# q of the first two units fetched two positions to a packet, with its decay factors in that order and ten more fillers on TensorE

## The chip, the core and the metric

The kernel runs on one core of a Trainium2 chip. A core has a matrix engine, TensorE (PE in the profile, its weight loads PEld), three engines for elementwise work, VectorE (DVE), ScalarE (ACT) and GpSimd (POOL), and SyncE (SP), which here only issues DMAs. Sixteen DMA engines move data between the chip's memory (HBM) and the core's on-chip memory of 128 rows (SBUF). TensorE writes its products to a second on-chip memory (PSUM), from where DVE or ACT take them. The engines run side by side and wait for one another on semaphores.

The metric is the device time in microseconds (us): the median of several runs. The profile is of one execution, and has times of its own.

## The reference

Two blocks follow one another. The first is a retention layer: for each of 8 batches and 8 heads, with 576 positions and 64 values to a head, scores are taken between q and k, multiplied by a decay and applied to v. The second is a gated feed-forward network without nonlinearity. All is float32.

```python
scores = scale * np.matmul(q, k.transpose(0, 1, 3, 2))        # scale = 1/sqrt(64)
gamma = 1.0 - 2.0 ** (-5.0 - np.arange(H))
Dmat = np.where(rel >= 0, gamma[:, None, None] ** rel, 0.0)   # rel = pos_i - pos_j
x = np.matmul(scores * Dmat, v)          # (8, 8, 576, 64), then laid out as (4608, 512)

a = x @ w1                               # 512 -> 1024
b = x @ w2
h = a * b @ w3                           # 1024 -> 1024
out = h @ w_out                          # 1024 -> 512
```

The weights come as float64 values. The kernel takes them as pairs of 32-bit integers and converts them itself.

## The kernel before, in words

**Units.** The retention is worked in units. A unit is a pair of batches and one piece of the positions; a pair has five pieces, the first of 64 positions and four of 128, so there are 4 x 5 = 20 units, numbered g. The decay gamma^(i-j) is split into a factor for q (`decay_q`, which has the scale in it) and one for k, which is applied to v (`decay_k`). Within a unit the full scores are computed and masked to j <= i; from earlier pieces comes a running state, k times v, kept in PSUM.

**The steps of a unit.** `load` (L87, its DMA at L93) fetches k, q or v of a unit into a tile with one position to each row of SBUF: a row holds, for 2 batches and 8 heads, 64 values, so every packet of the transfer is 64 values, 256 bytes. `scale` (L195, L204) multiplies q or v by its factor, on DVE, POOL or ACT. `front` (L207) turns k and q with PE transposes (L218), two heads at a time, into PSUM tiles `tp`, from which ACT copies (L221) them to `kT` and `qT`. `score` (L224) has PE compute the scores (L233), and DVE multiplies them by the mask (L236) into `pm`. `state` (L240) adds k times v on PE (L255), and ACT copies the state (L259). `pv_state` and `pv` (L264, L278) multiply q by the state (L274) and `pm` by v (L299); ACT copies the result (L306) into `xT`, the input of the network.

**The network.** `up` (L511) does the products with w1 and w2 by a scheme of seven products in place of eight (products at L528, sums on DVE at L533, the gate at L566). Its operands are sums of weights (`strassen_weights`, L149) and of tokens (`strassen_tokens`, L496). The weights are loaded in blocks (`load_block`, L342 and L345) and converted on ACT (L395 to L397) and DVE (L399, L402, L413, L426). w3 and w_out are multiplied together first (L477), and `down` (L632, L645) applies them. From about 200 us on the weights' sums are kept in HBM and fetched again for each group of tokens (`up2`, L1029, L1052).

**The order.** Each engine works its instructions off in the order in which the program writes them; nothing is rearranged. The tile framework adds the semaphore waits. Tiles come from pools with a fixed number of buffers, and a new tile waits until the buffer's last user is done. [...]The start of the program, which the change touches, is written out by hand: the loads of unit 0 (L97 to L100), the constants, the decay of q transposed to one position to each row (L117 to L125, tiles `dq`, `gps` and `gq`), then L726 to L770 with units 0 and 1, between them conversions of weights.

**Fillers.** `keep_busy(n)` (L127) issues n products of the identity with itself into a tile that nobody reads. A float32 product is two passes on PE, which the profile counts singly: 10 products at L119 are its x20.

Of the kernel before, what the change touches and what calls it, by code (L numbers as in the profile page):

```python
# [8 lines left out]
F32 = mybir.dt.float32  # L9
# [4 lines left out]
ALU = mybir.AluOpType  # L14
# [5 lines left out]
def kernel(  # L20
# [13 lines left out]
    nc = tc.nc  # L34
    moe_w1, moe_w2, moe_w3, moe_w_out = (
        w.bitcast(I32).rearrange("r (c t) -> r c t", t=2) for w in (moe_w1, moe_w2, moe_w3, moe_w_out))
    B, H, S, D = q.shape
# [3 lines left out]
    P = 128  # L41
# [6 lines left out]
    NC = (S + P - 1) // P  # L48
    short = S - (NC - 1) * P
    sizes = [short] + [P] * (NC - 1)  # L50
    starts = [0] + [short + c * P for c in range(NC - 1)]
    G = NB2 * NC
    NB = 3
    TB = S // NB
    NT = 2 * TB // P
    KD = DM // P
    KF = DF // P
# [4 lines left out]
    const = ctx.enter_context(tc.tile_pool(name="const", bufs=1))  # L62
    wp = ctx.enter_context(tc.tile_pool(name="wp", bufs=1))
    ffn = ctx.enter_context(tc.tile_pool(name="ffn", bufs=2))
# [6 lines left out]
    pools = {}  # L71
# [9 lines left out]
    acc = acc_part.enter_context(tc.tile_pool(name="acc", bufs=7, space=PSUM))  # L81
# [3 lines left out]
    live = {}  # L85

    def load(g, names, engine=nc.sync):  # L87
        i, c = divmod(g, NC)
        sz = sizes[c]
        src = {"k": k, "q": q, "v": v}  # L90
        for nm in names:
            t = pools["ld"].tile([P, 2 * H, D], F32, tag="ld_" + nm, name="ld_" + nm)
            engine.dma_start(  # L93
                t[:sz], src[nm][2 * i:2 * i + 2, :, starts[c]:starts[c] + sz, :].rearrange("b h p d -> p (b h) d"))
            live[nm, g] = t

    dq = ffn.tile([P, 4, 2, TB], F32, tag="c", name="dq", bufs=1).rearrange("p a b s -> p (a b s)")[:H, :S]  # L97
    nc.scalar.dma_start(dq, decay_q)
    load(0, "k")
    load(0, "q")  # L100

    ident = const.tile([P, P], F32, tag="ident", name="ident")
    make_identity(nc, ident)
# [19 lines left out]
    for c in (0, slice(1, NC)):  # L123
        n = short if c == 0 else P
        nc.vector.tensor_copy(gq[:n, c, :], gps[:n, c, :])  # L125

    def keep_busy(n):  # L127

        t = acc.tile([P, P], F32, tag="acc", name="idle")
        for _ in range(n):  # L130
            nc.tensor.matmul(t, ident, ident, start=True, stop=True)
# [63 lines left out]
    def scale(g, nm, scalar=False, engine=nc.gpsimd):  # L195
        c = g % NC
        sz = sizes[c]
        t, gam = live[nm, g], {"q": gq, "v": gk}[nm]
        t = t[:sz].rearrange("p (b h) d -> p b h d", b=2)
        if scalar:  # L200
            for h in range(H) if scalar is True else scalar:
                nc.scalar.mul(t[:, :, h, :], t[:, :, h, :], gam[:sz, c, h:h + 1])
            return
        engine.tensor_tensor(  # L204
            out=t, in0=t, in1=gam[:sz, c].unsqueeze(1).unsqueeze(3).to_broadcast([sz, 2, H, D]), op=ALU.mult)

    def front(g, names="kq"):  # L207
        c = g % NC
        sz = sizes[c]
        for nm in names:  # L210
            src = live[nm, g]
            dst = pools["fr"].tile([P, 2, NP, P], F32, tag=nm + "T", name=nm + "T",
                                   bufs=1 if nm == "k" and g >= NC else 2)
            for b in range(2):
                tp = acc.tile([P, NP, P], F32, tag="acc", name="tp")
                for p in range(NP):
                    h = b * H + 2 * p
                    nc.tensor.transpose(tp[:, p, :sz],  # L218
                                        src[:sz, h:h + 2, :].rearrange("p a d -> p (a d)"),
                                        ident[:sz, :sz])  # L220
                nc.scalar.copy(dst[:, b, :, :sz], tp[:, :, :sz])  # L221
            live[nm + "T", g] = dst

    def score(g):  # L224
        c = g % NC
        sz = sizes[c]
        kT, qT = live["kT", g], live["qT", g]
        pm = pools["fr"].tile([P, 2, 2, NP, P], F32, tag="pm", name="pm", bufs=1)
        for b in range(2):
            sc = [acc.tile([P, NP, P], F32, tag="acc", name="sc") for j in range(2)]  # L230
            for p in range(NP):
                for j, hs in enumerate(heads):
                    nc.tensor.matmul(sc[j][:sz, p, :sz], kT[hs, b, p, :sz], qT[hs, b, p, :sz],  # L233
                                     start=True, stop=True)
            for j in range(2):
                nc.vector.tensor_mul(pm[:sz, b, j, :, :sz], sc[j][:sz, :, :sz],  # L236
                                     mask[:sz, :sz].unsqueeze(1).to_broadcast([sz, NP, sz]))
        live["pm", g] = pm

    def state(g):  # L240
        c = g % NC
        sz = sizes[c]
        if c == NC - 1:
            return
        vs = live["v", g]
        kn = live["k", g]
        if c == 0:
            live["st"] = st_ps.tile([P, 2, NP, D], F32, tag="st", name="st")
        st = live["st"]

        for b in range(2):
            for p in range(NP):
                for j, hs in enumerate(heads):
                    h = b * H + 2 * p + j
                    nc.tensor.matmul(st[hs, b, p, :], kn[:sz, h, :], vs[:sz, h, :],  # L255
                                     start=(c == 0 and b == 0 and p == 0), stop=(c == NC - 2),
                                     skip_group_check=True)
        sb = pools["fr"].tile([P, 2, NP, D], F32, tag="sb", name="sb")
        nc.scalar.copy(sb, st)  # L259
        live["sb", g + 1] = sb  # L260
# [64 lines left out]
    def load_block():  # L325
        n = loaded[0]
        if n == len(blocks):
            return
        key, w = blocks[n]
        t = raw.tile([P, CV, 2], I32, tag="raw", name="raw", bufs=5)  # L330
        if key[0] in ("A", "w12"):
            if key[0] == "A":
                _, r, f = key
                t4 = t.rearrange("p (j c n) t -> p j c n t", j=2, c=2)
                parts = [(t4[:, j], w[:, f * P:(f + 1) * P]) for j, w in enumerate((moe_w1, moe_w2))]
            else:
                _, fp, _, r = key
                parts = [(t.rearrange("p (c n) t -> p c n t", c=2), w[:, fp * QC:(fp + 1) * QC])]
            for t2, src in parts:
                src = src[2 * r * P:2 * (r + 1) * P]  # L340
                if r == 0:
                    nc.sync.dma_start(t2, src.rearrange("(c p) n t -> p c n t", p=P))  # L342
                else:
                    for half in range(2):
                        nc.sync.dma_start(t2[heads[half]],  # L345
                                          src.rearrange("(c a d) n t -> a d c n t", a=2, d=D)[1 - half])
        elif key[0] == "wo":
            src = w.rearrange("(a i x) n t -> i a x n t", i=KF, x=BL)[key[1]]
            for a in range(QP):
                nc.sync.dma_start(t[a * BL:(a + 1) * BL], src[a])  # L350
        else:
            _, ft, h = key
            src = w[ft * P:(ft + 1) * P].rearrange("(j r) (a h f) t -> h a r j f t", r=BL, a=QP, h=DF // CV)
            for a in range(QP):
                nc.sync.dma_start(t[a * BL:(a + 1) * BL].rearrange("p (j f) t -> p j f t", j=P // BL), src[h, a])
        live["raw", n] = t
        loaded[0] += 1
# [105 lines left out]
    def convert(n):  # L463

        for _ in range(n):
            if go_on() is not None:
                return
# [105 lines left out]
    g = 0  # L573
# [152 lines left out]
    load_block()  # L726
    load(0, "v")
    load_block()
    load(1, "kq")
    load_block()  # L730
    load(1, "v")
    load_block()
    scale(0, "q", engine=nc.vector)
    front(0, "k")
    keep_busy(4)
    front(0, "q")
    convert(2)
    score(0)
    scale(0, "v")
    state(0)  # L740
    convert_up_to(1)
# [4 lines left out]
    convert_up_to(2)  # L746
    load_block()
    front(1, "k")
    keep_busy(4)
    scale(1, "q", engine=nc.vector)  # L750
    front(1, "q")
    convert(2)
# [392 lines left out]
    g = NC  # L1145
# [9 lines left out]
    for g in first_pair:  # L1155
        n = (1, 1, 2, 2)[g - NC]
# [38 lines left out]
    g = 2 * NC - 1  # L1195
# [10 lines left out]
    g = 2 * NC  # L1206
# [14 lines left out]
    for g in range(2 * NC, G):  # L1221
        n = dealt[g - 2 * NC]
# [42 lines left out]
    g = G  # L1265
# [44 lines left out]
```

## Time and profile before

Three runs took 835.63, 835.77 and 836.71 us; the median is 835.77. The profiled execution took 836.28 us by the same measure, of which 834.6 are the span of the profile.

| | busy us | share of the span | instructions |
|---|---|---|---|
| PE | 816.1 | 98% | 6095 |
| PEld | 735.5 | 88% | 6095 |
| DVE | 545.4 | 65% | 962 |
| ACT | 291.7 | 35% | 609 |
| POOL | 216.2 | 26% | 247 |

The core read 103.62 MB from HBM and wrote 22.28 MB. By stretches PE was busy for 25.38 us of the first 30, 27.25 of the next 30, 39.51 of the 40 after these, and 99.97 of the 100 from there. PE's mean clock was 0.994 of full over the span, and 0.83 in the first 30 us.

In the profile a line such as L233 is a line of the kernel before. `out<-in` names the tile written and those read; "xN" counts instructions of one kind that stand together; what stands in brackets after an instruction is the time for which its engine was idle before it, and what ended that. SPq and ACTq are the queues on which SP and ACT issue DMAs. "PEclk" is the clock that was granted to PE, as a share of full speed.

### The profile page before, as it was taken

The numbers are of one execution on the slowest core, as the hardware profiler recorded it, in microseconds if no ns is written. First come the engines' busy times: TensorE is split into PE (matmuls) and PEld (weight loads), VectorE is DVE, ScalarE is ACT, GpSimd is POOL, SyncE is SP. The second block draws the span as 40 slices with busy tenths as digits, with TensorE's granted clock in tenths as the row PEclk, the third lists the DMA queues.
The fourth block names the chain that finished last, engine by engine and source line by source line (L and its number), as shares of the span: only waits on it lengthen the run. The fifth ranks groups of instructions, "written<-read, shape, count | busy, mean of one in ns | idle before, by whom it ended". The sixth has DMA issues, their size and how long they took to land.

```text
span 834.6 us, 15774 instructions
## 1 busy us (share of the span) xinstructions
PE 816.1 (98%) x6095; PEld 735.5 (88%) x6095; DVE 545.4 (65%) x962; ACT 291.7 (35%) x609; POOL 216.2 (26%) x247
## 2 busy tenths in 40 slices
PE   7999999999999999989999999999999999999998
PEld 7889999744888998779999889998889998899987
DVE  4899999992554558754657755577745667646653
ACT  4787556581111011245453024342034331033300
POOL 1000000001102353005556105555006461045600
PEclk8999999999999999999999999999999999999999
DMA  9995464446035668997876537978245453046311
GB/s 195 222 220 138 78 142 132 114 119 109 6 76 120 101 162 285 278 291 193 211 226 178 109 80 206 223 238 221 57 96 177 159 195 114 34 149 215 139 30 47
DMA packets 197484, 126.96 MB, mean 152 GB/s; under 512 B 157848, under 2 KB 179096, under 8 KB 197408
## 3 DMA queue, kind: packets, MB, share of 16 engines
q1 hardware_dynamic: 168560, 50.40, 29.5%
q0 software_dynamic: 11824, 63.31, 23.0%
q10 hardware_dynamic: 17024, 12.23, 5.3%
q8 instruction: 48, 0.79, 0.4%
q14 instruction: 28, 0.23, 0.1%
HBM read 103.62 MB, written 22.28 MB: 151 GB/s over the span
## 4 chain that ended last, share of the span: by engine, by line
PE 83%; DVE 7%; DMA 6%; issue 2%; SPq 1%; ACT 0%; POOL 0%; ACTq 0%; DVEq 0%
PE po L645 21%; PE up L1052 17%; PE up L528 14%; PE seed L1052 13%; PE ps L477 7%; PE xps L299 3%; PE sc L233 3%; PE xps L274 1%; DMA ld_v<-in_v_dram 1%; SPq L171 1%; PE tp L218 1%; DMA out_dram<-ot 1%; DMA ld_q<-in_q_dram 1%; PE st L255 1%; DVE ab L1024 1%
## 5 line engine op out<-in xcount | busy, mean ns | idle before, releaser
L645 PE MATMUL po<-w3o,ab 128*128 128x256 f32 x552 | 125.1, 381 | 4.0 <-DVE ot L649 3.2
L645 PEld LDWEIGHTS po<-w3o,ab 128*128 128x128 f32 x552 | 103.7, 190 | 20.8 <-DVE ot L649 5.1
L1057 POOL TENSOR_TENSOR cc<-cc 128x384 f32<-128x384 f32 x112 | 109.3, 1002 | 3.8 <-ACT cc L1075 2.4
L1064 DVE TENSOR_TENSOR cc<-seed,cc 128x384 f32<-128x384 f32 x88 | 48.6, 552 | 69.1 <-PE seed L1052 60.1
L181 POOL TENSOR_TENSOR bl_q<-bl_q,gqs 128x512 f32<-128x512 f32 (+1 forms) x26 | 25.9, 1014 | 187.8 <-DMA bl_q<-in_q_dram 184.4
L1052 PE MATMUL up<-xT,ra 128*128 128x192 f32 x384 | 73.5, 328 | 0.0
L528 PE MATMUL up<-xT,wA 128*128 128x192 f32 x384 | 70.7, 328 | 0.8 <-DVE xT L496 0.8
L533 DVE TENSOR_TENSOR c<-up,c 128x384 f32<-128x384 f32 x80 | 44.0, 550 | 39.6 <-PE up L528 39.2
L236 DVE TENSOR_TENSOR pm<-sc,mask 128x512 f32<-128x512 f32 (+1 forms) x80 | 45.3, 627 | 34.9 <-PE sc L233 34.8
L1064 DVE TENSOR_TENSOR cc<-up,cc 128x384 f32<-128x384 f32 x88 | 48.4, 550 | 29.8 <-PE up L1052 21.8
L528 PEld LDWEIGHTS up<-xT,wA 128*128 128x128 f32 x384 | 63.3, 190 | 2.2 <-PE up L528 1.1
L645 PE MATMUL po<-wB,forms 128*128 128x256 f32 x288 | 65.1, 379 | 0.0
L1052 PEld LDWEIGHTS up<-xT,ra 128*128 128x128 f32 x384 | 63.8, 190 | 1.0
L645 PEld LDWEIGHTS po<-wB,forms 128*128 128x128 f32 x288 | 54.7, 190 | 7.4
L1071 ACT COPY seed<-up 128x384 f32<-128x384 f32 x56 | 25.9, 463 | 100.2 <-PE up L1052 55.2
L953 POOL DMA_DIRECT2D ra<-kept x53 | 30.0, 565 | 117.7 <-PE seed L1052 88.5
L477 PE MATMUL ps<-wo,w3T 128*128 128x512 f32 x128 | 55.1, 592 | 0.0
L1052 PE MATMUL up<-ra 128*128 128x192 f32 x288 | 54.7, 326 | 0.0
L1052 PE MATMUL seed<-e,ra 128*128 128x192 f32 x256 | 50.9, 329 | 0.0
L477 PEld LDWEIGHTS ps<-wo,w3T 128*128 128x128 f32 x128 | 24.3, 190 | 30.1 <-issue 29.7
L1052 PEld LDWEIGHTS up<-ra 128*128 128x128 f32 x288 | 48.1, 190 | 0.1
L528 PE MATMUL up<-T,wS 128*128 128x192 f32 x256 | 46.7, 326 | 1.4 <-DVE wS L149 1.4
(129 smaller groups left out, 1467.5 us busy)
## 6 DMA issues: line engine op xcount, KB each, us to landing
ra<-kept POOLq DMA_DIRECT2D x53, 896.0 KB, 5.0
raw<-in_moe_w_dram SPq DMA_DIRECT2D x72, 128.0 KB, 3.0
out_dram<-ot ACTq DMA_DIRECT2D x50, 128.0 KB, 2.3
bl_q<-in_q_dram SPq DMA_DIRECT2D x192, 32.0 KB, 3.1
bl_k<-in_k_dram SPq DMA_DIRECT2D x136, 32.0 KB, 3.3
raw<-in_moe_w_dram SPq DMA_DIRECT2D x16, 256.0 KB, 6.4
ld_k<-in_k_dram SPq DMA_DIRECT2D x8, 512.0 KB, 6.2
raw<-in_moe_w_out_dram SPq DMA_DIRECT2D x32, 128.0 KB, 2.7
```

Source lines behind the costliest of these rows:

```text
L181: nc.gpsimd.tensor_tensor(out=part, in0=part, in1=gqs[:, :, n0:n0 + n].unsqueeze(3).to_broadcast([P, NP, n, BL]), op=ALU.mult)
L233: nc.tensor.matmul(sc[j][:sz, p, :sz], kT[hs, b, p, :sz], qT[hs, b, p, :sz], start=True, stop=True)
L236: nc.vector.tensor_mul(pm[:sz, b, j, :, :sz], sc[j][:sz, :, :sz], mask[:sz, :sz].unsqueeze(1).to_broadcast([sz, NP, sz]))
L477: nc.tensor.matmul(ps, live["w3T", ft][:, g, :], live["wo"][:, g, :], start=(g == 0), stop=(g == KF - 1))
L528: nc.tensor.matmul(ps[:, w, :], a[:, w, r, :], b[:, r, :], start=(new and w == r == 0), stop=(w == r == 1), skip_group_check=True)
L533: nc.vector.tensor_add(c[:, to], ps, c[:, sb])
L645: nc.tensor.matmul(ps[nm], a[A][:, f, :], live["W"][B][:, f, :], start=(f == 0 and not on), stop=(f == NP - 1), skip_group_check=True)
L953: engine.dma_start(ring[n % 3], kept[n % 14 // 7][nm])
L1052: nc.tensor.matmul(ps[:, w, :], weight_of(slot, a, w), B[b], start=(new and w == 0), stop=True, skip_group_check=True)
L1057: nc.gpsimd.tensor_tensor(out=o, in0=o, in1=i, op=ALU.add)
L1064: nc.vector.tensor_add(c[:, j], ps, with_add[:, j])
L1071: nc.scalar.copy(p6, p1)
```

## The change

The change has four parts, all in the first units.

- q of units 0 and 1 is fetched by `load_pairs`: a row of SBUF now takes two neighbouring positions of one batch, so that a packet is 128 values, 512 bytes. Each unit's q takes two DMAs on SP, one for each batch, to 32 or 64 rows each; before, it was one DMA to 64 or 128 rows.
- The decay factors of q for these two units are needed in the same order. Four DMAs on ACT fetch them, ahead of the one for `dq`, into two tiles `dq2`; PE transposes them (four more transposes, two for each unit) into `gp2`, and ACT copies them to `gq2` (two copies).
- `scale` of q for these units no longer works in place. Two multiplies on DVE, one for the even and one for the odd positions, write to a new tile (`live["q2"]`), which has even positions in its first half and odd ones in its second. `front` transposes the halves one after the other, and ACT's copies put them back in the order of positions as they write `qT`: every second word for each copy. So both copies must be done before the first score, where before the first copy was all that the first batch's scores needed.
- After the scores of unit 0 there are five more products of `keep_busy`, ten passes on PE.

`dq2` takes buffers of the tag "T" and `q2` one of the tag "ab" in the pool `ffn`, ahead of their first users before.

```diff
+    def load_pairs(g):
+
+        i, c = divmod(g, NC)
+        n = sizes[c] // 2
+        t = live["q", g] = pools["ld"].tile([P, 2 * H, D], F32, tag="ld_q", name="ld_q")
+        for b in range(2):
+            nc.sync.dma_start(
+                t[b * n:(b + 1) * n].rearrange("p (h j) d -> p h (j d)", j=2),
+                q[2 * i + b, :, starts[c]:starts[c] + 2 * n, :].rearrange("h (i j) d -> i h (j d)", j=2))
+
     dq = ffn.tile([P, 4, 2, TB], F32, tag="c", name="dq", bufs=1).rearrange("p a b s -> p (a b s)")[:H, :S]
+    dq2 = [ffn.tile([H, 2, sizes[c]], F32, tag="T", name="dq2", bufs=5) for c in range(2)]
+    for c in range(2):
+        for b in range(2):
+            nc.scalar.dma_start(dq2[c][:, b], decay_q[:, starts[c]:starts[c] + sizes[c]])
     nc.scalar.dma_start(dq, decay_q)
     load(0, "k")
-    load(0, "q")
+    load_pairs(0)
...
+    gq2 = const.tile([P, 2, 2, H], F32, tag="gq2", name="gq2")
+    gp2 = acc.tile([P, 2, 2, H], F32, tag="acc", name="gp2")
+    for c in range(2):
+        n = sizes[c]
+        for j in range(2):
+            nc.tensor.transpose(gp2[:n, c, j, :], dq2[c].rearrange("h b (i j) -> h j (b i)", j=2)[:, j], ident[:H, :H])
+        nc.scalar.copy(gq2[:n, c], gp2[:n, c])
...
+        if nm == "q" and g < 2:
+            if not g:
+                live["q2"] = ffn.tile([P, 2 * KF, TB], F32, tag="ab", name="q2").rearrange("p f t -> p (f t)")
+            n = 2 * H * D
+            to = live["q", g] = live["q2"][:, g * n:(g + 1) * n].rearrange("p (h d) -> p h d", d=D)
+            for j in range(2):
+                engine.tensor_tensor(out=to[:sz, j * H:(j + 1) * H],
+                                     in0=t[:sz].rearrange("p (h j) d -> p j h d", j=2)[:, j],
+                                     in1=gq2[:sz, c, j].unsqueeze(2).to_broadcast([sz, H, D]), op=ALU.mult)
+            return
...
-                nc.scalar.copy(dst[:, b, :, :sz], tp[:, :, :sz])
+                if nm == "q" and g < 2:
+                    nc.scalar.copy(
+                        dst[:, :, :, :sz].rearrange("p b m (i j) -> p m b i j", j=2)[:, :, :, :, b],
+                        tp[:, :, :sz].rearrange("p m (b i) -> p m b i", b=2))
+                else:
+                    nc.scalar.copy(dst[:, b, :, :sz], tp[:, :, :sz])
...
-    load(1, "kq")
+    load(1, "k")
+    load_pairs(1)
...
     score(0)
+    keep_busy(5)
     scale(0, "v")
```

## The prediction

> **What bounds the kernel now.** I read the page first, then the chain of waits and the timeline of the first 45 us, then the stretches of the clock. The page says that TensorE (PE) is busy for 98% of the span, so only the start, where PE, DMA and VectorE (DVE) still wait for one another, can move:
>
> ```profile
> PE   7999999999999999989999999999999999999998
> PEclk8999999999999999999999999999999999999999
> DMA  9995464446035668997876537978245453046311
> ```
>
> Only the first slices of PE and of its clock are low, and the DMA engines are full there. In the chain of waits the first 24 us are not PE's work: they are a decay load, the queue of SP, and the load of q of unit 1.
>
> ```profile
> 2.04 5.64 DMA gk<-decay_k_dram
> 7.70 0.59 SPq L345
> 8.98 9.33 DMA ld_q<-in_q_dram
> 18.33 1.24 DVE ld_q L204
> 19.66 1.94 PE tp L218 x8
> 21.60 2.06 PE sc L233 x16
> 23.66 2.46 DVE pm L236 x4
> ```
>
> From there DVE is in the chain until PE's run of products begins at 31.06 (pm ends at 26.1, then conversions back to back). The timeline of PE, with the idle time before a piece and what ended it:
>
> ```profile
> 9.28 1.15 PE L233 MATMUL sc<-qT,kT 64*64 64x64 f32 x32 [0.21 <-ACT qT L221]
> 12.24 1.15 PE L255 MATMUL st<-ld_v,ld_k 64*64 64x64 f32 x32 [1.81 <-POOL ld_v L204]
> 16.80 1.91 PE L131 MATMUL idle<-ident 128*128 128x128 f32 x8
> 21.53 3.12 PE L233 MATMUL sc<-qT,kT 64*128 64x128 f32 x32
> ```
>
> There is a hole of 1.81 us behind the first scores, where the ten fillers go. The stretches by time (busy PE, PEld, DVE, ACT, POOL; granted clock; DMA share; GB/s) show what follows:
>
> ```profile
> 13.00:14.00 1.00, 1.00 (x35) 1.00 (x33) 0.96 (x3) 0.57 (x2) 0.00 (x0) 0.78 1.35 217
> 17.00:18.00 1.00, 1.00 (x7) 1.00 (x6) 0.66 (x1) 0.72 (x2) 0.00 (x0) 0.50 1.14 321
> 23.00:24.00 1.00, 1.00 (x14) 1.00 (x14) 0.36 (x1) 0.97 (x2) 1.00 (x1) 0.60 1.00 234
> ```
>
> The clock falls to half in the first of these (stretches of 0.1 us put it at 13.57) and comes back in the last (23.80). At half clock eight filler passes take 1.91 us, where they took 1.16 at 7.27, and the 32 score passes of a 128-row unit 3.12, where unit 2's take 2.06. The GB/s are those of k of unit 1 (256-byte packets) in the first line, and of weights in 1 KB packets over 128 rows in the second.
>
> [...]weights in 1 KB packets to 64 rows (the four of L345, 9 to 12 us) moved at 183 to 243 GB/s.
>
> **The change, part by part.** I add against the profiled 836.28 us (span 834.60 and 1.68 around it); the median of the three runs, 835.77, lies 0.51 below.
>
> *Queue order.* [...]Before, five loads of SP went out without a wait (0.81 to 4.4 us). The change puts five more DMAs into the first ten: four of the decay on ACT, one more of q on SP. The second half of q(0) now waits for k(0), which lands 4.2 us after its issue, at 5.0; before, all of q(0) went out at 1.60. Behind it on SP stand, at 0.65 each, the two weight loads (2.30 to 5.7), v(0) (3.79 to about 7.1) and everything else. First bytes come 1.5 us after an issue, so DMA is dry from about 4.4 (k(0) and half of q(0) moved) to 6.5. By 6.4 us the kernel before had moved 0.77 MB; the changed one has moved 0.45. The 0.32 MB at 290 GB/s cost 1.1 us of the DMA stream.
>
> *Packets.* q(0) and q(1) become 512 and 1,024 packets, from 1,024 and 2,048. From 18.9 ns for a 256-byte packet on one of 16 engines (217 GB/s) and 53 for 1 KB (310), a straight line gives 30 for 512 bytes: q(1) 1.9 us, from 2.4. But the halves go to 64 and 32 rows, and 64 rows moved 183 to 243 GB/s even in 1 KB packets, hence 2.2 to 2.9 us. Bounds for q(1): 1.2 us gained (packets cost the same at 512) to 0.5 lost; I take 0.2 gained. The stream is then 0.9 late from q(1) on, 1.0 at v(0) and k(1).
>
> *ACT and PE at the start.* Four DMA issues of 0.59 put the table load (1.28) to about 5 to 6.4 and dq to 3.25; both are just in time for the transposes at 6.0. They are covered by the first fillers, which end at 6.07; a contended small load took 3.9 us (gk), so dq could come 0.9 late. Then four more transposes (0.13 each by the five at L122), with ACT's copy of the first pair (0.17 by L125, and two hand-overs) between them: 0.9 on PE ahead of k's transposes. With fillers of 1.0, q(0)'s transposes start at 9.05, from 8.36. The multiply of q(0), two of about 0.65 for one of 1.22, starts when the second half has landed, about 7.8, and so ties with that. Scores of unit 0 wait for both copies of qT: 10.3, from 9.28.
>
> *Fillers.* Five calls are ten passes: 1.45 us at full clock (1.16 for eight), 2.4 at half. The hole moves with v(0): 11.2 landed, 1.9 of POOL, state at 13.15 instead of 12.24. Scores end at 11.5, so 1.45 fits; at half clock it would add 0.7.
>
> *Unit 1.* ACT's second conversion stands behind the state's copy, so it is late by the same 0.9; DVE's L413 waits for it, and q(1)'s multiply stands behind that: 18.33 becomes 19.2, from the DMA side (0.9) as well. From the multiply to pm took 5.31. Now it is 1.30 (two halves), 0.1, second half of the transposes, 0.65 (a copy that now writes every second word; 0.59 before, no slower row to bound it[...]), 0.1, first half of the scores: 3.7 us at full clock (0.52 and 1.03), 5.2 at half (0.97 and 2.06). Does the clock hold? [...]So I take a drop at 20.4. If it returns at 23.8, the span is 4.95 and pm 0.5 late; [...]at half clock until 27.2 pm is 0.75 late, and the slower products with v (L274, 1.10 at full clock) push PE's first product from 28.77 to about 30.6, its successor, 1.5 later, to 32.1: 1.0. Between 0.5 and 1.0 I take 0.7.
>
> *What is late next.* DVE's chain to 31.06 is dense, so this goes to PE. The fourth weight block (ACT L395 waits 0.45 for it at 24.86) lands 0.9 late; ACT's next two steps end at 28.05, xT's copies at 29.2, and the first product starts there, from 28.77: 0.4, inside the 0.7. The next block (L395 at 34.88, 1.79 of waiting) is 0.9 late, and through ACT's dense row to 41.3 so are unit 2's scores; PE has 1.42 us of waiting for DVE at 55.53, which takes that up. Later tiles change places only.
>
> Sum: 1.1 − 0.2 = 0.9 of DMA; at pm 0.9 − 0.36 to 0.1 (the way to pm of 4.95 to 5.2 against 5.31) = 0.5 to 0.8; at the end 0.5 to 1.0, taken as 0.7: 837.0 profiled, **836.5** beside the median.
>
> **Rivals.**
> 1. *The fillers keep the clock full through unit 1's scores.* For: the hole is filled. Against: the wait for q(1)[...]. pm at 22.9, 0.7 early; but xT's copies wait for the late block, the first product starts at 29.2 and its successor at 30.7, 0.4 early: 835.4.
> 2. *Packets of 512 bytes cost what 256 do, and k(0) lands sooner.* q gains 1.5, the stream is 0.4 early, and with a full clock DVE's chain 1.0 to 1.8 early: 834.8 to 834.0. Against: the 64-row rate. This alone could reach faster by over 0.2%.
> 3. *Slower: half-row transfers.* If 512-byte packets to 32 and 64 rows move at the 150 GB/s of 4 to 6 us (q(0), 64 rows), q(1) takes 3.5 us, 1.1 more; the multiply starts at 20.5 and, at half clock, pm at 25.7: 2.0 late, 837.8. It decides from a multiply later than 20.1.
> 4. *The loads hide the split altogether* (k(0) lands at 4.3, nothing dry): within 0.3 of before, 835.8.
>
> **Chances.** Forecast 0.36, rival 1 0.14, rival 2 0.10, rival 3 0.28, rival 4 0.12. What a measurement tells from no change is 0.2%, 1.7 us. The forecast spreads by about 1 us (dq 0.9, the copy 0.6[...]), so 0.06 of it crosses to slower, and of rival 2 a little stays within: faster 0.09; same 0.57; slower 0.34. Range 834.7 to 838.7: from rival 2's nearer end to rival 3 with dq's 0.9 on top. The likeliest case alone is 835.5 to 837.5.
>
> **What would show it.** SP's second issue of q(0) near 5 us, with low GB/s from 4.5 to 6.5; v(0)'s multiply on POOL after 11; the SP row of packets 1,536 fewer; unit 0's scores at 10.3; the clock at half for part of 20 to 24; pm of unit 1 at 24.1 to 24.4. Wrong: q(1) landing before 18.3, a clock full from 10 to 24, or L533 waiting longer after 31 us than before.

## The result, and the profile after

The changed kernel took 844.21 us (median of six runs, 840.62 to 848.30); the kernel before, run beside it, 836.11 (six runs, 834.74 to 838.19). The ratio is 1.0096, with a 95% interval of 1.0075 to 1.0118: 8 us slower. The prediction said 836.5, with 838.7 as its upper end. The profiled execution of the changed kernel took 848.30 us (span 846.6), the slowest of its six, so its trace shows more loss than the median has; a second profile, of 841.56 us, comes with the experiments.

The page of the changed kernel, the same three rows of slices as before (each slice is now 21.2 us):

```profile
PE   8899999999999998899999999999999999999998
PEclk9899999999999999989999999999999999999999
DMA  9994464446035669896976626979255453145401
```

PE is still at 98% of the span, but there are new weak places: the clock in the second slice (21 to 42 us), PE in the sixteenth and seventeenth (317 to 360), and the clock again in the eighteenth (360 to 381). The prediction looked for nothing so late.

The chain of waits of the changed kernel, from 14 us to the multiply of q(1) (start, duration, what):

```profile
14.04 2.43 PE idle L152 x10
16.47 1.40 PE st L291 x32
...
18.37 0.79 ACT e L431
...
20.70 0.70 DVE e L449
...
22.03 0.70 DVE q L226
```

Before, this stretch belonged to the load of q of unit 1, which ended at 18.33. Now no DMA is in it, and the ten fillers are: the state waits for them on PE, ACT's conversion (L431 to L433) waits behind the state's copy, DVE's step L449 waits for the conversion, and the multiply of q(1), which stands behind L449 on DVE, starts at 22.03.

The timeline of PE with the same pieces as before:

```profile
12.07 1.97 PE L269 MATMUL sc<-qT,kT 64*64 64x64 f32 x32 [0.47 <-ACT qT L253]
13.97 2.50 PE L152 MATMUL idle<-ident 128*128 128x128 f32 x10
16.40 1.44 PE L291 MATMUL st<-ld_v,ld_k 64*64 64x64 f32 x32
24.85 3.79 PE L269 MATMUL sc<-qT,kT 64*128 64x128 f32 x32 [0.70 <-ACT qT L253]
```

The scores of unit 0 take 1.97 us, where they took 1.15, and the fillers 2.50. By the durations that is half clock: in the profile of before eight fillers took 1.91 us at a granted 0.50, and 1.16 earlier. The hole of 1.81 us that the fillers were to fill does not exist in this execution: v(0) is ready before they end. The stretches (busy PE, PEld, DVE, ACT, POOL; clock; DMA share; GB/s):

```profile
13.00:14.00 1.00, 1.00 (x21) 0.88 (x17) 0.71 (x2) 0.97 (x2) 0.91 (x1) 1.00 1.33 223
17.00:18.00 1.00, 1.00 (x38) 1.00 (x38) 0.21 (x1) 0.11 (x1) 0.00 (x0) 1.00 1.17 202
23.00:24.00 1.00, 1.00 (x8) 0.67 (x7) 0.97 (x3) 0.47 (x1) 0.00 (x0) 0.95 0.65 196
```

The clock column has 1.00 in the first row although the durations say half. The first change that the column shows is at about 23.9, and ahead of a first change it is no evidence; by the durations PE comes to full clock at about 17.1. From 23.9 to 30.7 the clock is at half again.

The loss does not end there. I compare when PE starts the scores of each unit. Unit 0 is 2.79 us late against the profile of before, unit 1 3.32, unit 2 3.82, units 3 to 8 (50 to 298 us) 3.9 throughout. Then unit 9 is 7.37 late, unit 10 9.14, unit 11 11.98, and so it stays to the end. So in this execution a third of the loss (3.9 us) arises in the first 50 us, and two thirds (8.1) between 298 and 399. The timeline of PE at the scores of unit 9, before:

```profile
317.27 2.06 PE L233 MATMUL sc<-qT,kT 64*128 64x128 f32 x32
```

and after:

```profile
324.64 3.49 PE L269 MATMUL sc<-qT,kT 64*128 64x128 f32 x32 [3.38 <-DVE kT L211]
```

PE stands still for 3.38 us. In its last 0.4 us the granted clock falls from 1.00 to 0.50, to come back between 327.5 and 328.0, and the scores take 3.49 us. It waits for `kT`, which DVE makes here from a tile `bl_k` that sixteen small DMAs of SP fill (L192). The chain of waits has the last of these, before:

```profile
308.95 5.29 DMA bl_k<-in_k_dram
```

and after:

```profile
312.98 10.05 DMA bl_k<-in_k_dram
```

Beside these loads run POOL's writes of the weights' sums to HBM (`kept`, L932 and L935). The DMA engines are full from about 306 us before and from about 310 after, but do not move the same. Taking the 15 us that begin 15 us after the scores of unit 8, before:

```profile
308.96:323.96 15.00, 15.00 (x152) 13.77 (x151) 10.98 (x16) 2.05 (x6) 10.66 (x15) 1.00 1.06 352
```

and after:

```profile
312.88:327.88 15.00, 11.62 (x130) 11.02 (x128) 6.40 (x10) 1.68 (x5) 6.48 (x9) 0.89 1.04 314
```

The same kinds of transfers, the same busy share of the DMA engines (1.06 and 1.04; the measure can pass 1), and 314 GB/s where it was 352. The question for the experiments was why.

### The profile page after: what moved, and what is told of

The parts are those of the page before. It is cut to its first block, busy times and chain, and to the rows that moved or that the text cites. A ratio compares the mean times of both kernels' runs of the same rounds, so it can differ in the third digit from the quotient of the medians.

```text
span 846.6 us, 15816 instructions
## 1 busy us (share of the span) xinstructions
PE 825.7 (98%) x6109; PEld 743.3 (88%) x6109; DVE 544.9 (64%) x964; ACT 292.2 (35%) x611; POOL 216.6 (26%) x247
## 4 chain that ended last, share of the span: by engine, by line
PE 85%; issue 6%; DVE 4%; DMA 2%; ACT 1%; SPq 1%; POOL 0%; ACTq 0%; DVEq 0%; POOLq 0%
PE po L681 21%; PE up L1090 17%; PE up L564 15%; PE seed L1090 13%; PE ps L513 6%; PE sc L269 4%; PE xps L335 3%; PE xps L310 2%; PE st L291 1%; PE tp L249 1%; DMA bl_k<-in_k_dram 1%; SPq L192 1%; DVE ab L1062 1%; PE idle L152 1%; PE idle L133 1%
## 5 line engine op out<-in xcount | busy, mean ns | idle before, releaser
L202 POOL TENSOR_TENSOR bl_q<-bl_q,gqs 128x512 f32<-128x512 f32 (+1 forms) x26 | 25.9, 1016 | 187.6 <-DMA bl_q<-in_q_dram 183.1
```

The source lines that it names most:

```text
L202: nc.gpsimd.tensor_tensor(out=part, in0=part, in1=gqs[:, :, n0:n0 + n].unsqueeze(3).to_broadcast([P, NP, n, BL]), op=ALU.mult)
```

## The experiments

All were timed in five rounds with the kernel before beside them, whose median was 836.2 to 837.9 there; the ratios are those of the record to these runs, and not quite the quotients of the medians. "Late at unit 8" is when PE starts the scores of unit 8, against the profile of before (293.96); "at the end" is the end of PE's work (831.15). "GB/s" is that of the 15 us named above, and "last k" the time from issue to landing of the 256 KB load of k in it. These four are of one profiled execution each, which can lie far from the median: e2's, with 841.71 us, was the slowest of its fourteen. f1 and f2 move the writes out of that stretch, so they have no entry there.

| run | kernel, edit | median us | ratio, 95% | late at unit 8 | at the end | GB/s | last k |
|---|---|---|---|---|---|---|---|
| before | | 836.11 | | 0 | 0 | 352 | 8.4 |
| changed | | 844.21 | 1.0096 (1.0075 to 1.0118) | 3.92 | 11.89 | 314 | 17.8 |
| e1 | changed, no fillers | 844.45 | 1.0099 (1.0070 to 1.0128) | 1.56 | 9.34 | 313 | 17.8 |
| e2 | before, fillers | 836.08 | 1.0002 (0.9984 to 1.0019) | -0.63 | 5.42 | 342 | 14.5 |
| e3 | changed, no decay loads | 846.52 | 1.0101 (1.0063 to 1.0140) | 4.18 | 13.54 | 311 | 17.5 |
| e4 | before, PE held up at 92 us | 842.05 | 1.0065 (1.0045 to 1.0085) | 2.23 | 5.19 | 351 | 8.3 |
| f1 | changed, writes later | 846.04 | 1.0114 (1.0091 to 1.0136) | 2.61 | 8.18 | | |
| f2 | before, writes later | 840.06 | 1.0037 (1.0023 to 1.0050) | -0.71 | 1.56 | | |
| f3 | changed, again | 844.25 | 1.0082 (1.0061 to 1.0103) | 2.78 | 5.14 | 306 | 20.1 |
| f4 | before, short warm-up | 838.60 | 1.0019 (1.0002 to 1.0036) | -0.64 | -1.67 | 346 | 8.3 |
| g1 | before, left side +128 bytes | 843.01 | 1.0066 (1.0042 to 1.0090) | 0.34 | 6.49 | 312 | 17.9 |
| g2 | changed, left side +128 more | 841.52 | 1.0057 (1.0035 to 1.0079) | 3.35 | 7.05 | 347 | 12.4 |
| g3 | before, left side +256 | 837.85 | 1.0016 (1.0001 to 1.0032) | -0.30 | -0.83 | 349 | 7.7 |
| g4 | before, right side -224 | 835.33 | 0.9995 (0.9981 to 1.0009) | -2.09 | -2.67 | 352 | 7.9 |
| h1 | changed, +128 more, no fillers | 838.69 | 1.0011 (0.9995 to 1.0027) | 0.82 | 3.47 | 351 | 15.2 |
| h2 | before, q in two transfers | 835.57 | 0.9998 (0.9980 to 1.0015) | -0.02 | -1.27 | 354 | 10.9 |
| h3 | before, left +256, right -480 | 835.28 | 0.9989 (0.9969 to 1.0010) | -1.71 | 0.02 | 353 | 7.6 |
| h4 | changed, left +128 more, right -480, no fillers | 836.18 | 0.9998 (0.9981 to 1.0014) | -1.00 | -0.17 | 355 | 8.0 |
| i1 | before, left side +64 | 843.28 | 1.0065 (1.0040 to 1.0090) | -0.08 | 5.50 | 314 | 17.6 |
| i2 | before, right side -32 | 836.32 | 0.9984 (0.9965 to 1.0004) | -0.49 | -0.44 | 346 | 15.7 |

### First: the start, and whether lateness alone is enough

Four runs took the change apart by its visible pieces. e1 leaves the fillers out of the changed kernel:

```diff
     score(0)
-    keep_busy(5)
```

> The changed kernel without its five products of keep_busy behind unit 0's scores. In the changed kernel these ten passes ran at half clock, from 13.97 to 16.47 us, and the state of unit 0 started at 16.40 although v was ready at 13.90. If the fillers cost the time (theory F), the state starts near 14.0, unit 2's scores come about 1.4 us later than before instead of 3.8, and the median is 2 to 3 us below the changed kernel's. If the queue of SP sets the start (theory Q), DMA is as late as in the changed kernel, q(1) is multiplied no earlier than about 21, and less than 1 us is gained. If the clock is what counts (theory C), leaving the fillers out lets the clock come to full later than 17.1 us and nothing is gained or it becomes slower. In all three the stage from 297 to 399 us, which took 8 us more in the profiled run of the changed kernel, is open: if it goes by how late the start is, it shrinks with it.

e2 puts them into the kernel before:

```diff
     score(0)
+    keep_busy(5)
```

> The kernel before with only the five products of keep_busy added behind unit 0's scores. Scores end at 10.43 us there and v is ready at 12.18. Theory F: the passes cost only what does not fit into the hole, 0 us at full clock (1.45 into 1.81) and 0.6 at half; within 0.7 us of before. Theory C: they keep the clock at full past 13.57 us, scores of unit 1 take 2.06 us and not 3.12, and the kernel is 0.3 to 1.0 us faster. Theory Q: no difference, since no DMA changes.

e3 keeps the changed kernel's fillers, and makes `dq2` from `dq` by copies on DVE in place of the four loads on ACT:

```diff
-            nc.scalar.dma_start(dq2[c][:, b], decay_q[:, starts[c]:starts[c] + sizes[c]])
...
+            nc.vector.tensor_copy(dq2[c][:, b], dq[:, starts[c]:starts[c] + sizes[c]])
```

> The changed kernel without its four DMAs for the decay: four copies on DVE take the decay from dq instead, and the rest stays (pairs of positions, two multiplies, fillers). SP's loads of unit 0 up to the two weight loads then go out without waiting for k(0). Theory Q: q(0) has landed by 6.5 us, the two weight loads by 8.5, v(0) goes out at about 5 to 5.5 us instead of 6.54, the state of unit 0 starts 1 us or more earlier, and 1 to 3 us of the 8 are gained. Theory F and theory C: the fillers and the late clock stay, and less than 1 us is gained.

e4 only makes PE late, far from the start, in the kernel before:

```diff
+    keep_busy(16)
     up(0, 0, 2, conv=[2, 1, 1, 2, 2], tail=False)
```

> The kernel before with 32 filler passes (keep_busy of 16) ahead of the first products of up for the third piece of tokens (near 92 us), which delays PE by about 3.9 us there, as the changed start does, and changes nothing before it. If the stage from 297 to 399 us loses time because everything reaches it 3.9 us later (theory S), the median is 7 to 9 us above before. If that loss has to do with the changed kernel's own DMAs or is chance, the median is 3.5 to 4.5 us above before.

Without the fillers the start recovers 2.4 us (1.56 late at unit 8, from 3.92; a second profile of the changed kernel, f3 below, has 2.78), but the median nothing (844.45). In the kernel before, the fillers cost nothing (836.08). The timeline of PE in e2 shows why:

```profile
10.45 1.38 PE L131 MATMUL idle<-ident 128*128 128x128 f32 x10
12.47 1.15 PE L255 MATMUL st<-ld_v,ld_k 64*64 64x64 f32 x32 [0.64 <-POOL ld_v L204]
```

At full clock they take 1.38 us, and 0.64 of the hole is left. So the prediction's sum for them was right for the clock and the start that the kernel before has. In e1, free of the fillers, the load of q(1) is in the chain of waits again:

```profile
10.48 2.34 SPq L103
...
12.86 7.20 DMA ld_q<-in_q_dram
...
20.15 0.70 DVE q L226
```

It lands at 20.06. The forecast was 19.2, from 18.33. With the decay loads gone, e3 is as late as ever (4.18 at unit 8), so they are not what holds the start; whether they cost anything beneath the fillers, e3 can't tell.

e4 makes no use of anything in the change. Its passes hold PE up by 3.9 us (in its profile unit 4 is 1.64 early, with nothing edited before it, and unit 5 is 2.24 late), and it costs 5.4 us (836.5 times 0.0065). That is more than the forecast of 3.5 to 4.5 for lateness that is only passed on, and less than the 7 to 9 of theory S: by the medians, lateness costs some 1.5 us more than itself. It was tempting to stop here; but e1 is less late at unit 8 than e4, and loses more.

### Second: are the writes in the way of the block loads?

f1 and f2 move the first writes of `kept` two products later, in the changed kernel and in the one before; the diff is the same:

```diff
-            todo.extend([*ups[:2], forms[0], *ups[2:], forms[2], (flush,), forms[1], (down, (1, 0), (1, 1)),
+            todo.extend([*ups[:4], forms[0], *ups[4:], forms[2], (flush,), forms[1], (down, (1, 0), (1, 1)),
```

> The changed kernel, with the first weights' sums of the late stage formed and written back two products later, so that POOL's sixteen writes no longer run beside the sixteen block loads of k of unit 9. Theory L (collision: at 297 to 325 us those writes and the block loads share the DMA engines; a start that is 1.5 to 4 us late turns that into a wait of PE of 3.4 us and a fall of the clock): no idle ahead of unit 9's scores (under 0.5 us, where the changed kernel had 3.38), full clock from 320 to 330, the shift of unit 9 the same as that of unit 8 within 0.5, median 837 to 840.5. Rival R (it is no collision; the late stage loses in any case, by its new slots): idle of 3 us or more stays, median 842 to 846.

> The kernel before with that same edit alone. Theory L: its late stage was just in time already (no idle ahead of unit 9's scores in its profile), so the fastest runs stay at 834 to 835, the slower ones of 837 to 840 get fewer, median 834 to 836. Rival R: no difference, 836 with the same spread; if the later writes hit the stores of the output at 330 to 350 instead, 838 to 841.

The wait at unit 9 is gone, as theory L said: in f1 unit 9 is 2.61 late, like unit 8. And nothing is gained. In f1's timeline of PE:

```profile
346.49 3.56 PE L681 MATMUL po<-w3o,carry 128*128 128x256 f32 x8 [4.89 <-ACT ot L715]
```

PE now waits for a tile that a store of the output must free. The kernel before loses 3.1 us by the same edit (1.0037). So the collision is real, but the kernel before has it too, and moving it is worse. L explains where PE waited, not why the changed kernel waits more.

f3 repeats the changed kernel, for a second profile. f4 shortens the warm-up ahead of the first transposes in the kernel before, to see what a longer half clock at the start costs:

```diff
-    for _ in range(10):
+    for _ in range(6):
```

> The changed kernel once more, nothing edited, for a second profile of its start. Theory P ([...]how long PE stays at half clock at the start is chance): full clock begins at another time than 17.1 us, unit 0's scores 1.0 to 2.8 later than in the kernel before, unit 2's 1.5 to 4.2; median 842 to 846. Rival (the edit itself keeps the clock half): full clock at 17 again, unit 0's scores 2.7 to 2.9 late, unit 2's 3.8 to 4.2.

> The kernel before with six instead of ten fillers ahead of the first transposes, no other edit: they end near 4.2 us[...]. Theory C (a late full clock at the start is what costs): full clock not before 8 us and in most runs not before 10; unit 0's scores 0.8 to 2 late, unit 2's 1 to 3, and the late stage adds its 3 to 6: median 838 to 843. Rival D (the DMA stream sets the start, the clock there is covered): unit 2's scores within 0.5 of the kernel before, median 835.5 to 837.

In f3 the start's loss is 2.78 at unit 8, with the clock at half from 8.2 to 15.1 and from 21.9 to 28.7; the fillers, again:

```profile
12.94 2.38 PE L152 MATMUL idle<-ident 128*128 128x128 f32 x10
```

It has no wait at unit 9 and loses 2.4 us after unit 8, where the first profile lost 8. When the clock falls differs from run to run: at 23.9 us in the first profile of the changed kernel, at 21.9 in this one. f4's profile had half clock from 8.5 to 18.7, and f2's, whose start is that of before, until about 20 by the durations; yet unit 1's scores stood at 21.08 and 21.55, against 21.53. So in these two profiles of the start before, a bad clock is covered by the load of q(1), against theory C. But f4's median, 838.60, lies 2 us higher, where C had put it (838 to 843) and not its rival (835.5 to 837), in runs from 833.93 to 844.87. Its one profile is of an execution of 834.60 us and doesn't show where the longer ones lose, so C is not excluded for those.

### Third: where the tiles lie in SBUF

The 15 us at 309 to 324 had a pattern by then: 306 to 314 GB/s in every profile of the changed kernel and its kin (changed, e1, e3, f3), late or not, and 342 to 352 in every profile of the kernel before and its kin (before, e2, e4, f4). So I compared the addresses that the two programs give to their tiles. The new tile `gq2` is 128 bytes long in each row, and comes from the pool `const`, which lies ahead of the pools on the left side of SBUF. In the kernel before wA begins at 18176 bytes, 71 times 256, and wS, xT, T, `ab`, `ot` and `carry` at multiples of 256 as well. In the changed kernel each lies 128 bytes higher. Only wA and wS, the sources of the `kept` writes, take part in the transfers of these 15 us.

g1 gives the kernel before that displacement and nothing else. A constant tile, of which two words are used, is made 128 bytes longer; no instruction differs. g2 does it to the changed kernel, so that its left side comes to a multiple of 256 again:

```diff
-    lim = const.tile([P, 2], F32, tag="lim", name="lim")
+    lim = const.tile([P, 34], F32, tag="lim", name="lim")
```

> The kernel before with one constant tile 128 bytes longer (32 words that nobody reads), so that the tiles allocated after it on the left side of SBUF (weights wA and wS, xT, T, ab, ot, carry) lie 128 bytes higher, at 128 beyond a multiple of 256, as in the changed kernel, whose added tile gq2 has that size. No instruction differs. Theory A (place in SBUF: the DMA engines move these tiles more slowly from there): in the 15 us that follow 15 us after unit 8's scores 300 to 320 GB/s where the kernel before had 349 to 356; the late stage loses 2 to 8 us and the start nothing: median 838.5 to 843. Theory S (only the late start of PE makes the late stage lose): no difference, 836 to 837.3, and 326 to 382 GB/s there.

> The changed kernel with that same longer tile, so that the tiles after it lie 256 bytes higher than in the kernel before, and at a multiple of 256 again. Theory A: the start is as late as in the changed kernel (2.6 to 4.2 us at unit 2), the late stage moves 330 to 380 GB/s and loses no more than in the kernel before: median 838 to 841. Theory S: as the changed kernel, 843 to 846.

g1's stretch:

```profile
309.30:324.30 15.00, 11.36 (x126) 10.75 (x126) 6.14 (x10) 1.68 (x5) 6.76 (x10) 0.85 1.04 312
```

its timeline of PE, at unit 9:

```profile
321.32 3.79 PE L233 MATMUL sc<-qT,kT 64*128 64x128 f32 x32 [3.64 <-DVE kT L190]
```

and g2's stretch:

```profile
312.31:327.31 15.00, 15.00 (x152) 13.77 (x151) 10.98 (x16) 2.05 (x6) 9.55 (x13) 1.00 1.06 347
```

The displacement alone makes the kernel before slower by 5.5 us (1.0066), with the changed kernel's own wait at unit 9, 3.64 us, out of a start that is only 0.34 late. Taken out of the changed kernel, it gives back the 347 GB/s and the undisturbed unit 9, and the median falls to 841.52, between the ranges of theory A (838 to 841) and theory S (843 to 846).

The wait at unit 9 alone is no mark of the displacement. e2's profiled execution has it too, with everything in place and at 342 GB/s:

```profile
321.24 3.78 PE L233 MATMUL sc<-qT,kT 64*128 64x128 f32 x32 [4.52 <-DVE kT L190]
```

f3, which is displaced, does not have it. What all displaced kernels share is the rate of this stretch. Nor is it the engines that read the displaced tiles more slowly: the 552 products of L645 take 381 ns each before and 383 in g1, and the loads of the sums (`ra<-kept`, 896 KB each, into displaced tiles as well) land after a median of 5.0 us in both.

In the DMA view of these 15 us (size, then us from issue to landing) the load of k shows it best, before:

```profile
ld_k<-in_k_dram SPq DMA_DIRECT2D x1, 256.0 KB, 8.4
```

and in g1:

```profile
ld_k<-in_k_dram SPq DMA_DIRECT2D x1, 256.0 KB, 17.9
```

g3 and i1 ask from which distance on this counts. The same tile is made 256 bytes (66 words) and 64 bytes longer (18 words):

> The kernel before with that tile 256 bytes longer: the tiles after it lie at a multiple of 512, where they lay at 256 beyond one. Theory A in its wide form (the larger the power of two, the faster): 833 to 836; in its narrow form (a multiple of 256 is all that counts): 836 to 837.3, like theory S.

> The kernel before with the constant tile 64 bytes longer (left side at 64 beyond a multiple of 256). If what counts is a multiple of 256: 305 to 318 GB/s in the 15 us of block loads and writes, as with 128 bytes, the last load of k landing 17 us or more after its issue, median 840 to 844. If what counts is a multiple of 64: 342 to 355 GB/s and 835.5 to 838.

64 bytes spoil as much as 128 (314 GB/s, 843.28, unit 9 waits 4.66 us), and at 256 the rate is whole again (349). So of the distances tried, 64 and 128 bytes beyond a multiple of 256 spoil the rate and 0 does not. g3's median is 1.3 us up all the same, with an interval that just excludes no change, in runs from 834.41 to 843.85; why is open. Of all eighteen profiles with an entry in the column GB/s, the six with a displaced left side have 306 to 314 GB/s and a last load of k of 17.5 us or more; the twelve others have 342 to 355 and 7.6 to 15.7.

Why the distance counts is not shown. By the program, `kept` takes a row of wA in runs of 128 values, 512 bytes; the profile has these writes in larger packets (3.5 KB on average, 1338 for 4.71 MB in the 15 us of the kernel before), so it says nothing of the runs. And 64 bytes off cost no less than 128: 314 and 312 GB/s.

### Fourth: the other side, and what is left of the change

The right side of SBUF holds the loads of q, k, v and the raw weights. There every tile, in both kernels, lies 224 bytes beyond a multiple of 256. g4 and i2 leave 224 and 32 bytes free at the upper edge, in the kernel before, by a pool opened ahead of the others there:

```diff
+    edge = ctx.enter_context(tc.tile_pool(name="edge", bufs=1, side="right"))
+    edge.tile([P, 56], F32, tag="edge", name="edge")
```

(56 words in g4, 8 in i2.) h3 leaves 480 bytes (120 words), and has the left side 256 bytes up as in g3.

> The kernel before with 224 bytes left free at the upper edge of SBUF, so that the tiles of its right side (loads of q, k, v, raw weights, kT, qT, pm), which lie at 32 bytes beyond a multiple of 64, lie at a multiple of 256. Theory A in its wide form: the loads go faster, at the start too; median 832 to 835.5. Narrow form or theory S: 836 to 837.3.

> The kernel before with 32 bytes left free at the upper edge of SBUF (right side at multiples of 64, where it was at 32 beyond). If what counts for the loads is a multiple of 64: q(1)'s multiply at 16.3 to 17.6 as with 224 or 480 bytes free, DMA 240 GB/s or more from 4 to 6 us, median 834.5 to 836. If it is a multiple of 256: multiply at 18.2 to 18.7, 150 to 160 GB/s, median 835.5 to 837.5.

> The kernel before with 480 bytes left free at the upper edge of SBUF and the constant tile 256 bytes longer, so that both sides lie at multiples of 512. Theory A in its wide form: the loads of the start are as fast as with 224 bytes free (q(1)'s multiply at 16.3 to 16.8) or faster, the late stage at 350 GB/s; median 833 to 835.5. Narrow form: no more than the luck of a profile, 835.5 to 837.5.

The stretch from 4 to 6 us, in which k(0) and q(0) are under way; before:

```profile
4.00:6.00 2.00, 2.00 (x11) 1.77 (x10) 0.00 (x0) 0.00 (x0) 0.00 (x0) 1.00 1.34 154
```

i2, at a multiple of 64:

```profile
4.00:6.00 2.00, 2.00 (x15) 1.88 (x14) 0.00 (x0) 0.00 (x0) 0.00 (x0) 1.00 1.32 160
```

g4, at a multiple of 256:

```profile
4.00:6.00 2.00, 2.00 (x13) 1.88 (x12) 0.00 (x0) 0.00 (x0) 0.00 (x0) 1.00 1.16 254
```

h3 has 230 there. Again the multiple of 256 is what gains: 224 bytes off it the loads move 154 GB/s, 192 off (i2) 160, in place 254 and 230. Why is not shown here either; the displaced side is the one written, where in the late stage it was the one read. In g4's timeline of DVE the multiply of q(1) starts at 16.48, from 18.33, in h3 at 17.59, and in neither does it wait for q any more:

```profile
16.48 1.22 DVE L206 TENSOR_TENSOR ld_q<-ld_q,gq 128x1024 f32<-128x1024 f32 x1
```

The start is 2.09 us early in g4 and 1.71 in h3. That is little more than luck can do: e4 was 1.64 early at unit 4 with nothing edited before it. What is shown is the faster loads. Of the early start the whole keeps 0.4 and 0.9 us by the ratios (medians 835.33 and 835.28), and neither interval excludes no change: no version is shown to beat the kernel before.

h2 tries the extra places in SP's queue by themselves, with q of the two first units in two transfers of the old packets to all rows:

```diff
+            if nm == "q" and g < 2:
+                for b in range(2):
+                    engine.dma_start(t[:sz, b * H:(b + 1) * H],
+                                     q[2 * i + b, :, starts[c]:starts[c] + sz, :].rearrange("h p d -> p h d"))
```

> The kernel before with q of units 0 and 1 each fetched by two DMAs, one for each batch row, into all rows in the old packets of 256 bytes; nothing else differs. If the extra places in SP's queue cost by themselves: q(1)'s multiply starts 0.5 to 1 later than 18.33, median 836.5 to 838. If the loss of the stream comes from the four decay loads ahead of it and from the transfers to half the rows: 18.0 to 18.6, median 835.5 to 837.

They cost nothing: the multiply of q(1) starts at 18.30, and the median is 835.57. h1 and h4 leave the fillers out of the changed kernel and put the tiles in place, on the left side (h1: 34 words, as g2) and on both (h4: the right side 480 bytes down as well):

> The changed kernel with the longer constant tile (left side at a multiple of 256 again) and without the ten fillers: what is left of the change is q in packets of two positions, its four half transfers, the four decay loads and their transposes. Theory A + start: unit 1's scores 1.0 to 2.2 later than in the kernel before (q of unit 1 lands near 20, from 18.3), 340 GB/s or more in the 15 us of block loads and writes, median 837 to 839.5. If the later start alone costs the late stage as much as the displacement does: 840 to 843.

> The changed kernel without fillers and with both sides of SBUF at multiples of 512. If the packets of 512 bytes pay once the place in SBUF is good: q(1)'s multiply before 16.5 and a median below that of the kernel before with both sides so placed, 832 to 834.5. If the half transfers and the queue still hold it back: multiply at 17.5 to 19, median 1 to 2 us above that one, 835 to 838.

h1's median is 838.69, with a ratio whose interval includes no change (1.0011, 0.9995 to 1.0027). Its load of q(1) is still late, in the timeline of DVE:

```profile
20.19 1.29 DVE L226 TENSOR_TENSOR q<-ld_q,gq 128x512 f32<-128x512 f32 x2 [0.79 <-DMA ld_q<-in_q_dram]
```

h4, with 836.18, is at the level of the kernel before. Its multiply starts at 18.57, 0.98 later than in h3, which has the old packets in the same places. In both it stands behind DVE's step on the weights, which waits for ACT (2.00 and 1.71 us), and not for q: with the loads in place there is nothing left at this point for the packets of two positions to gain.

So the 8 us have two causes, which overlap. From the changed kernel, the displacement is worth 3.3 us (1.0096 to 1.0057 times 836; 2.1 from f3's 1.0082), and with that gone the fillers 3.8 (to 1.0011). By the intervals each of these differences is uncertain by 2 to 3 us. From the kernel before, the displacement costs 5.5, and the fillers nothing (e2). With the displacement there, taking the fillers out gains nothing (e1). It looks as if each of the two is enough to bring the late stage out of step, and the second then adds less; the runs show the sums, not that reason.

What stays open: why lateness alone costs as much as in e4 and g2. Both have 347 GB/s or more and no wait at unit 9, and lose a further 2.6 to 2.8 us between the scores of units 10 and 11, where PE is at half clock (367.8 to 374.6 in e4, 369.7 to 376.5 in g2). h1 and f3 lose there as well, f4, g3 and h2 nothing. PE waits there several times for 0.3 us, among transposes, for ACT, which scales q head by head (L202 of the kernel before). The kernel before, f4 and h2 don't have these waits; g3 has two of them, and no fall. What makes the clock fall in some of these profiles is not shown; and why e4 lands between 841.3 and 843.4 in all six runs, which chance would not do, I can't say.

## Why the prediction was wrong

**Queue order: right in place, too large in amount.** SP's second issue of q(0) waits 2.9 us for k(0) in the changed kernel and ends at 5.5, and DMA is nearly dry from 4 to 6: 43 GB/s, from 154. What makes it wait for k(0) is not shown, only that the dry stretch is gone without the four decay loads (150 GB/s from 4 to 6 in e3). The 0.32 MB at 6.4 us were less: from the rates of the 2-us stretches, e1 has moved 0.21 MB less by 6 us, and 0.23 by 8.

**Packets: wrong.** q(1) was to land 0.9 late, with 0.2 gained by its packets. Without the fillers in the way it lands at 20.06 in e1, from 18.31, and its multiply starts at 20.15 there and 20.19 in h1: 1.8 late. h2 excludes the split as such. In these single profiles the dry stretch is the smaller part: e3 has none, and its second half of q(1), issued at 12.97, still lands at 19.61. The rest comes with transfers of 512-byte packets to half the rows, and which of the two it is no run parts.

**Start on ACT and PE: right.** 10.3 was forecast for the scores of unit 0, and e1 has 10.37. In the changed kernel's two profiles they start at 12.07 and 11.04, with PE at half clock: the eight fillers ahead of them took 2.07 and 1.71 us, and 1.16 in e1.

**Fillers: the step that failed at the start.** "Scores end at 11.5, so 1.45 fits" took full clock for granted. The fillers took 2.50 and 2.38 us at half. I had the price of that, 0.7, but not what is queued behind: state, ACT's copy, ACT's conversion, DVE's L449, and only then the multiply of q(1). It starts at 22.03 and 20.58, for 19.2, with q(1) no longer the last to arrive.

**Clock and pm of unit 1.** A fall at 20.4 and a return at 23.8 or 27.2 were forecast, which were the author's estimates; it fell at 23.9 and 21.9 and came back at 30.7 and 28.7. What sets these times is not shown. The kind was right, and pm at 26.96 and 25.91, for 24.15 to 24.4, is mostly the late multiply. The 0.7 us at the end of the start became 2.8 to 3.9.

**"Later tiles change places only": the step that failed most.** The places were the cost. I had looked at which buffers the new tiles use, and for `gq2`, the one tile that got a place of its own, not at where it pushes the others. Nor did the forecast reckon with the writes of `kept`: with them moved (f1), the wait of 3.38 us at unit 9 is gone. The displacement, priced at nothing, is 5.5 us in the kernel before (g1). And the forecast ended its sum at unit 2, as if a start that is late by some us were late by the same at the end: e4, with nothing of the change in it, paid 5.4 for 3.9 us of passes.

**Rivals.** The slower one named half-row transfers, 837.8, from a multiply later than 20.1. Its condition was met and its sign right, but by h1's ratio its price is about 1 us, which isn't clear of none; it did not bring the 8. And its 150 GB/s were not the rows: g4 loads the same 64 rows in the same packets at 254, from a better place. Rivals 1 and 2, the faster ones, fall with the half clock and with q(1) at 20.06, rival 4 with the dry stretch.

## What to carry to other kernels

Before a small constant tile is added, see what is allocated after it: if tiles that DMAs read or write move off a multiple of 256 bytes, transfers can slow down far from the edit (from 352 to 312 GB/s at 309 us in g1, by a constant tile longer by 128 bytes), and a padded tile mends that (347 in g2). An instruction that is meant to fill a hole has to be priced at the clock that the hole may get (the ten fillers took 1.38 us in e2 and 2.50 in the changed kernel), and followed through the queues of all engines behind it. And when a start is late, look at the later stages with the fullest DMA, since the lateness can grow there (from 3.9 us at unit 8 to 7.4 at unit 9 in the changed kernel's first profile).

## What the runs showed of the hardware that was not expected

A left side displaced by 64 or 128 bytes made full DMA engines move 306 to 314 GB/s for 342 to 355, and a load that itself was not displaced landed after 17.5 to 20.1 us for 7.6 to 15.7, beside writes that were. A right side moved down by 224 or 480 bytes to a multiple of 256 raised the first loads from 154 GB/s to 254 and 230; moved down by 32, to 160.

One build's runs spread more than the difference between many edits: f4 has 22 runs from 833.93 to 844.87, and the kernel before, beside i1, 34 from 834.77 to 845.06. A single profile can't stand for such a build; the first one of the changed kernel lost 8 us after unit 8, the second 2.4.
